# Second-level sums for blocks 3 to 6 of the first layer in the second pair-of-batches pass, and a new instruction sequence

## The chip, the core and the metric

The kernel runs on one core of one Trainium2 chip. A core has a matrix engine (TensorE, PE in the profile, with its weight loads shown as PEld), a vector engine (VectorE, DVE), an activation engine (ScalarE, ACT), a general engine (GpSimd, POOL) and a queue that issues transfers (SyncE, SP). Each engine runs its own instructions in order and waits on semaphores for the others. The metric is the time of one execution on the device, in microseconds. The kernel before was timed in three runs, 1473.35 to 1478.22 us, median 1473.81.

## What is computed

Attention with normalised queries and keys, and then a two-layer product with a bilinear middle, all in float32:

```python
# q, k, v: (8, 12, 448, 64)
q_n, k_n = rmsnorm(q, g_q), rmsnorm(k, g_k)
scores = q_n @ k_n.T / sqrt(64)
attn = softmax(scores)
x = (attn @ v).transpose(0, 2, 1, 3).reshape(8 * 448, 12 * 64)   # 3584 x 768
a = x @ w_a                # 768 -> 1536
b = x @ w_b
out = (a * b) @ w_out      # 1536 -> 768
```

## The kernel before

**Attention.** Twelve heads of eight batches are taken in 24 steps p, each with four heads (in the code a step is a pair of head pairs). `loads` fetches q, k and v (line 424), `normalize` makes the root mean squares (lines 462, 464, 497, 499 on ACT, DVE and POOL), `transposes` turns k and q on TensorE (530) and copies them to a tile "qkT" (548, 550), `scores` multiplies and exponentiates (588, 594) into tiles "ET", `values` multiplies with v (610), `add_up` and `sums_over_keys` make the denominators (624, 646), and `invert` and `divide` apply them (696, 739). The result of a step is written into tiles "x", the input of the two-layer product. There are nine such tiles, four "ET", two "qkT", and one or two each of "q", "k", "v", "sq", "sum", "rec" and "qn".

**The two-layer product** runs over four passes beta = 0 to 3, each of two batches (896 tokens). The matrices are cut in 2 x 2 quarters, and seven products of sums of quarters take the place of eight plain ones. The sums of the weights' quarters are made once, in pass 0, and kept in DRAM ("kept" and "kept_o"); those of x are made by `combine`. The first layer is made in 12 units: six blocks m = 0 to 5 of 128 columns, each with ab = 0 (w_a) and 1 (w_b).

In passes 0 and 1 a unit is `quarter_products`: seven sums times three TensorE products of 448 columns (line 1295, tile "pq"), whose results are taken out of PSUM by ACT and DVE (1317 to 1352) and multiplied on POOL (1343, 1355). The unit's factors, 1.376 MB, are read from "kept" into one of two tiles "st" (393).

In passes 2 and 3 the first layer is `deep_products` instead: each of the seven products is cut once more, in 11 TensorE products of 224 columns (line 872, tiles "da" and "dg"), for w_a and w_b of a block together. A step (m, f), one of 6 x 7, needs factors from "kept" and from "kept_s"; three transfers fetch them (850 to 852) into one of four slots in the two "st" tiles. Sums of x's blocks, "dT" (835), stand in the four "ET" buffers, "sum", "rec" and "qn" for the whole layer; results are gathered in "dF" tiles (885, 891, 911, 912, 919, 924), which stand in the buffers of "q", "k", "sq" and "v", are summed (895) and multiplied (900) into "hT".

What "kept_s" holds is made by `deep_factors` (807): while pass 1 has both units of a block in "st", DVE makes five tiles "ds" of 896 columns in "ET" buffers, and SP writes each to DRAM (809).

The second layer of each pass is `last_product` (line 996, tile "po"), in passes 2 and 3 partly `inner_products` (1193). Its factors come from "kept_o" (395), and its results leave through "o_sb" or "oi" (1368). In pass 1, `inner_factors` makes factors for the later passes too (1132, 1134).

**What sets the order.** Every operation is recorded in a plan with what it reads and writes. `Plan.run` issues them in a fixed sequence, the string `ORDER`, which was made outside the kernel and keeps every operation behind what it depends on. Names such as "held", "ended", "deep factors" or "firsts1" are hints (`HINT`) and make no wait on the chip. The recording order matters where buffers rotate: a tile takes over the buffer of an earlier one of its kind. `PREP` is pass 1, `ONCE` pass 2, `DEEP` holds passes 2 and 3, and `HELD` is attention step 15, the first whose result finds no free "x" tile until pass 1's first layer is done.

In the profile the first output products of pass 0 stand near 407 us, pass 1's first layer from 524 to 717, pass 1's second layer beside attention steps 15 to 23 until 942, pass 2 until about 1196 and pass 3 after it.

Of the kernel before, what the change touches and what calls it, by code (L numbers as in the profile page):

```python
# [12 lines left out]
FP32 = mybir.dt.float32  # L13
# [7 lines left out]
def _float_of(bits):  # L21
# [11 lines left out]
    "c-rkZ33OFOmba>2z4y1bzrW_^X9WZi2#d0afb@VOwk)Hl;0^%=5+ETV3JD;KU}OzzfUt>S6SF|r6PB<f5kWR-MYcw9qaDHNwx@ee-<JfTTYE-5"  # L33
    "<D8xztA4%r>ej8h)xEdw7dtU}6~u~YLMZWqYI@CpMNGpoOt0b(7{qAjRdnpCg1-egK!(^^o)~b03)}(cl;Gq5I3AtQrk|8;!dSy-k=3_FX7dNl"
    "jE8!{nfKGu(|Vp9K}MwZ0G13e2nNHzXP<*-pMmV0oXNX#VA8mWTfHkLY=+V|td*|=&o9Vdx(@y`bN%AXg@sV~1~?b2qzelmZ|Sn7B=65K5@ydD"
    "`G*nnVMgAZuVBWk+^e}uKZhlsuD+7H^3@fKSHiOM%Q(@O<ewEjIAeaW7S5=r3-eCGi8XZ2>#L!VxU1KY<$qpIVEM8?EZf_5@7HjB=e1qsuzmUg"
    "vg7KGt;V*Basj69DuqzVE+AW9K7+EA!YMd)@^~>EJ67Z@ehW6O1K7BB_XcstH+y&NfonT%FW<&V*;V*rJ3wg}S%F)Z7cJkk_2S!Sw{P=Qmz_C$"
    "x~%Nv;Z2nXkHOJ5;hjGo+51i9#yxxXUf;9lz=M0gtlWQf&wKkeR%|>`0p)LB{Al;?YB=0#{h^%)cOE#sVaNXc>-QhqcWB?ygOxEgl{NdS_nkis"
    "hqn7bEIVkF?XQGg@-EMwU2uIj?EGTK?>+;e<daWIoBXMyj9j_AWy_`Omo9C&^5vD^esS^h;)}(fd}^M*qMrZwf_(n+N3P2kN~KHZN<U-gzWDIN"
    "D<2mZfBb>^+m9}NbNSMx*rJQSDK2_%^Xapj&wWtzzFGAC`z7a#E_yB%U2v3~J$Lr#2Sr6kjvYT;bmGJ}CyyTg_oAAk*RCD;ebK)a)m#hzuI9^A"  # L40
    "XHI=qZGL*9>SR^%yN3@SK6?Jhx#RB~K6dnQO-<3M>i?)YRQ2xftE#K3e)H8=iPcr_)fClK7kzp{Ir!<pw<`7hZymjG0$|fID2K|8u=DiJ>XT4$"
    "ctyoKaHOLAdO4KuKGX!(9RR=+DuX?jYsxAvZYeqc(W=YmHm_3muPVXK%g+>-6a#U?_VrtrmTg#Dco5beT6=Kq7FYtGFW$Io$zoWy7>r8*^XHvg"
    "Na@@KbLYPYr`P2XI6env!K|4ubH>{axb|8u<i1L#PX~Zk046Iruw@clfC;V%<6%5xL-sg)7)I8ZEP%|6EK1YU(?_RMnl=guj7SAY84kmTnI?fD"
    "L$YDWU`l}ue2xG-^E5pD6g>4LJoN<9?%y9ChyIU3KX^p;JPduIZy)H>8=%)i@DLb10eZmwJ;;58bnk{rLDzfX-Y(FkGjt(_aW_B*Xy2|~2hx_@"
    "1#o8@fYz;`RZD1@1W7F{q}~*6Z%UdF()c!ebAv=kOn`)VNI=0O0MX%aI6|Xn=o}3NDS+R%9(-N^%LEg2T}J{shChHSCnpDTAbUbKj4Ob#OUH_1"
    "VeCsU6XTeWl{xk$@x_cW85zRpbPzCJ(JsPEFnsv%S94#5P1A>sXG2Axsi|2b(nqAF4jGY}vLrM0?a3J_DKH@|W%$Ao!(rawVZ#O|zmRMV88jFM"
    "4H`HBhUW|(n>-{r`MJTF$<GahLC@$<r#!0+8>a9%{P|e}h75R8?w>rM|6@;iwm<sh#77^0`0>a3Ir|NGq_4AY9~o`=i05HJ==Vb3K0@!_LhtUq"
    "9_rrx*Fw*3&paSW{hsL8PwLv$A@R<fcj?syI`!z%sZ;m+I(6&TrE{l_y*d_j?AYlZ;clTr_YU`U_*J)Gb?DZ$Lx(P1x^(E)`Cqzr?%c)Q{+{;5"
    "?skIaYUdK=QFn<BM@#X(=3?_^f^=^S-n0{M(vbs`SlhOY3D_Zt3X~ASY6m0|r~L)Ms67<4IEXm@1QZ0O5k_zH>&*L=5M^0G%1o0}%2e$PqcTHs"
    "*hFTCT;wq#uZ$MB5X*%?fH3A4m`S`AGwc*^cShDAJ5F_uSP?FS5f_mK!RP0K7cq&+bUL|?B~m7}VygBmHMI^JiVjg4vKTcjlTlqCcLVufkv`!D"  # L50
    "ZnEcL#I)Z5pC4(Ml$g4K(V!BrJ8BE4yw2imqu?V(V8KvOVE$%|d3|Un3v79HK~ah9`6CIt-QN)Mhp!2}CP{=T?CLm=fQ(4`sFd^+GGgRVl98H1"
    "&OA@Z3ull%9SqOHz-I<R)pJmF2o4;Cqm`#<B|Rio9o^gi$iDqGk5^RDYBXK{gP39;dAz|RpKPtzD(vRMmd(Pp507lyTw1od^u0c%rw$0ckN0`^"
    "UCuZ4dh^Y9Hg2ryCH(s9l9K)FcI<_s3bLWFCs|*zcIyLW7YbqZxgKkZ#Wia-t%g%;VCBkpw>j2seP{K`)hl0LxnkAw$`#8Gu2{Yf3f8SHcw>7("
    "VPRSKH!gQ8C94Q@UAbuWq7552EL*>>_rj%1dgmWmvaEDTe$~=d1#jik%EdH4zoKH^qTP!Z&Fc#DSHZlzy!Bg_u3NEe`Letvd2>!JUa~lU_1q<k"
    "7A;@2qNbqJvVvumuwX&{0+_#W{;q{H=WoAf9+bTXn`f8I&dpsg^X?gWuf8^S?wt8+U+*wGZ~EP{XHK7fctyd?yO&O*`7>$xjP`lcb6=S~dDhfU"
    "Q(h~5rFhDesne!SnmlQ0VPS_UbmHoct6rWsvE$V7ujEc?H)&e_<ViV`U(P9?H!*J#%bqZP{9O~qPtBp(lcsFUp1k4Z?1|Zh6S8x%?_9O&rLiks"
    "LXWv~OjcITm@(rPjUSgiu6*3MaWm%5p3!z@=8W7sGp4`Qdd!PilgEq^AZttpj7m?>O)vN;{l#hN`B|9@&y8*~|Lo{_X=$UzjvV=7){7&@jD%Ol"
    "W<u&{Ou8^JJtHkGJ$+BgsLZsK%(V23(Jj+zhF6b*W{?W0L!n8Np+lY@oG~~#Ic-#0@~Gsr5y`2kxRRQZGAOl4%D|!622Q&JQ{2Mrrt@#ZqNU-$"
    "CmK#1@N`2V^J#b@9TG<k7&%~g|6%=yCc?0Icp)L~`9Xsoj;DPYjXW7kAq?Tiq8`0JItoH02oUu5^grN7hi}ioYusrVos4?`OikB7#RyP6NuCxS"
    "k9xc3uG-uRs?#Z>Pewf4iJK(KIle4Vl?IA6M@dqB(Y~-@s#uh1c3oyErlzQk6%#8oElJZ=OH~Xdpdi4PWN5mMKYQvk_11=^D~6#271ghpdK>&S"  # L60
    "OhpZAilQ63ua&O&6(8=4G9rel>j7Q2n(J1SsR#YK?rnu2uVRD^O$n-oY50s5s%5FB8qou)r76A^hNdc-qG_tnr>m-_>Sl8#<X04>t%`J2#Ri4("
    "9W<5J$P<~F(a74T>rt&OpXD=j!wex`pVeA7{d$a1$4ynS0@W<7nWY#ZMGK(HN|NDI?7g_4`c|5%s<zbXX0{53)*59uBFGWh1vI;O^)*)_MwVqL"
    "5#5W3E&YbBgjLhjL)e3=sW&(9p{Qu8TG<q@(p2jaLIP+|%eJJYMJZ@It=7~nmF5QWS5?1VG`CTF8qxG<T~=fpL-r}M*OUXd%d)2V+gJuZHME&&"
    "XnsGcqG>I3*;J!cSqUp<$V^fUuW8AuEc+E%w(zaUs@~*nJy0#%`k)PyRM|k<NLsE{Pd0T~m(_@jy2+L-8_i?{g)~hzeP&BjAMI0RHH5}PbLlOK"
    "A*iZbSKW$$TwH$Q(VR|&Yuq8Z6N%x}Dfci@6&op{!{rb)Q4(cA;_`!{$R(Z2T!|$Ov_zuD$i(j<#N~ELnnWbQLs$bs;z?W_iH#*Z5{bkT5);9^"
    "9VF$UKwR5k=WvkvX=2N$=y0<@R3ID(#s>XyG(asPMWPHVK4{z#<fKW!AMkU(SB=DZ4a*97Rnrhqc81B{rxK5>Bzk1Gi9>NmC4}9E+anvqaw#so"
    "AtMeq@kq?$aJob$Nut*!d0pJ4aSfb_4H(|Cu}Tbg;6)}dPN;peVlflP1g9Xhvu|6014wvf;El^zD?(WV$wA{KDOM6&iP3UQOhAloFB0x2K{e?0"
    "JA77@6><>C%b1?Tn4uYx7IeyPh5(nt?O>`?a&YcW6kXh*q9I)(=ez-P36iJ^f-DFQy!9G!j)qo{B~v7KV~H~dHw;`u09Q~}hZ&CyMCRsNV;6Ty"
    "E{@yrl6NqN<Y*`fPQo}-P-cmX4MjIMIDSw}9}49f6&&`ZEJsV6y0Jc>tf4?T<%rI)5}~{i?z8V_g-X1!D7u|4&Z#8fT=1x>!_&ZFI9#Graymqm"
    "iJ~~1Q66z_r|!nog&j9bROEu2N^dwD+Qou{VIAV3RKn_{5i*kmB^MECQ$%!%q9jRzi1aCSGwPvk2i0RKRXH*i8*%Cs&}xbxaHp%^Z2~fNB2$qu"  # L70
    "50hMtBnj2#g2)6sL!{tDZgIAPD1wtZIBkfeMNU0+THS`#4T!p3z34<C=)#E>abdMURir9$;$cqal$ac0UvMWA8(oo@C^0lBMFrek^fVC7Q=*F!"
    "k;ojW2*j>67>{sLP9>Zm2Zk<SFHk4hh%V?7Xd+rxB}BICEDQoEo=BW4h{ZTZH%(v;DvAPk2~SanFo4w>j7At9&~OozN<<az$0OwEn7olFI$ciP"
    "wjxbp#6_Cd5w%^|L1|d@5Vw<<4zwB-o3%hwxCn8?6OusU;}c?HFc=*?j*!?G+!r8`kUu^?==1qnwD3iOcldpwCV?RFhW-91e=ryoxx?!V`(ymR"
    "C_l4&{@8e5j1`G^V=Sw46uZY~n*IQ>;z)vJ#bCF*x*0G7je?f!HMBUdnP3K@6HIC{B}yYvh8m=b;rA+*8Ba8~-xG~@j^<N>iHha5b1UX{J(Q#c"
    "v}T&p%&TZYs@*2UX?X9c_DvBoH5cYOOLgfk681SmYKY3j=i_dV*x2AMg9%!^lz`zA(n!D=#T`D@82zFlp1Ok8ry&|7B;Y233!|2?gct^(L`aB$"
    "1MgS|a06TdV4S&J0B+0%3`1YAGXU150tmI$soe<t!!`1~pFfQZ`GJgn)Y{)J{$wV0qdx|I3y{*AfZ9{7<%It{?7trNqjpN{K}hYR_6>G~*}oeD"
    ">`^-*b=Ws>Y2EHR2-Hn$G3&m`cWM6>i+UorF5PT@3!wGDdiHf(NWDT(&&UP|H}*oUgm6>BTS-IxraJj30J(MBw}i>JM!WeSH{j%!17zPl)bE4-"
    "X!ri-YV;=|&|6)Zeh(HpcYTA}QHMlpcimWn`pi}bruBHVo^pM>++3tLkiLc1%W;#}Up4qUaC(y&+z<<Ha;CS+@U1BHzqAScyIw-R3nV|qzsOJZ"
    "Q9}M3Wb#u&f&4)E$j==`KUZ9me^kMKY5!~q_WxxgKU*M?UxM<N_J2NC(Eo*aBmcv3@-s!(FG2fD`{C^`Cf^JG"
# [68 lines left out]
def kernel(  # L148
# [35 lines left out]
    nc = tc.nc  # L184
# [90 lines left out]
    def fast_body(ld, wk, ps_s, ps_o, ps_mm, dram):  # L275
# [14 lines left out]
        DEEP, PREP = (NB - 2, NB - 1), NB - 3  # L290
# [474 lines left out]
        def firsts(beta):  # L765
            names = names_of(beta)
            key = 1e4 + beta * 1e3
            h = tile_of(f"h{beta}", "hT", 1)

            def open_h():  # L770
                hTs[0] = wk.tile([P, KO, 2, S], FP32, tag="hT", name="hT")
            op(None, 0.0, 0, open_h, [], [f"{h}/{m}" for m in range(KO)] + [f"{h}/open"], new=[h])
            if beta in DEEP:
                deep_products(beta, key, names, h)
                return
            for n, (m, ab) in enumerate(order):
                if beta:
                    stream(beta, n)
                    st, at = f"st{beta}.{n}", (beta, n)
                else:  # L780
                    st, at = f"st{n}", n
                quarter_products(beta, key, m, ab, st, at, names, h)
                if beta == PREP and ab:
                    deep_factors(beta, m)
# [7 lines left out]
        def deep_factors(beta, m):  # L792

            st, ts = [f"st{beta}.{2 * m + ab}/0" for ab in range(2)], {}
            w = lambda ab, c: (lambda: sts[beta, 2 * m + ab][:, :, c * P:(c + 1) * P])
# [3 lines left out]
            for n, x, y, alu, reads in ((0, w(1, 0), w(1, 1), ALU.add, []), (1, made(0), w(0, 0), ALU.subtract, [0]),  # L799
                                        (2, w(0, 0), w(1, 0), ALU.subtract, []), (3, w(0, 1), made(1), ALU.subtract, [1]),  # L800
                                        (4, w(0, 2), w(1, 2), ALU.subtract, [])):
                nm = tile_of(f"dk{m}.{n}", "ET", 4)

                def emit(n=n, x=x, y=y, alu=alu):
                    ts[n] = wk.tile([P, 2, S], FP32, tag="ET", name="ds", bufs=4).rearrange("p a b -> p (a b)").rearrange(
                        "p (f n) -> p f n", f=7)
                    nc.vector.tensor_tensor(ts[n], x(), y(), alu)
                op("DVE", 1.05, -0.5, emit, st + [f"dk{m}.{x}" for x in reads], [nm, "deep factors"], new=[nm], lock=True)
                op("SP", 0.43, 0, lambda n=n: nc.sync.dma_start(kept["s"][:, m, :, n], ts[n]), [nm], [f"ks{m}.{n}"], kb=434)

        def deep_products(beta, key, names, h):
# [30 lines left out]
            def step(m, f, F, names_F):  # L842
# [64 lines left out]
                if m == f == 0:  # L907
                    rest_of_a()
# [665 lines left out]
```

## Time and profile before

| | us | share |
|---|---|---|
| median of three runs | 1473.81 | |
| the profiled execution, on the device | 1477.19 | |
| its span, first to last instruction | 1475.2 | 100% |
| PE busy | 1452.8 | 98% |
| PE weight loads busy | 944.5 | 64% |
| DVE busy | 998.3 | 68% |
| ACT busy | 438.1 | 30% |
| POOL busy | 332.6 | 23% |
| mean DMA rate over the span | 167 GB/s | |

The profile is of one execution and lists for each engine when it worked. Matmuls are pipelined and their ends are modelled, so busy time of PE says that it was not waiting for long, not that it ran at its peak. A float32 product appears as two records. A row of the groups names a line of the code, the engine, the tiles, the shape and the number of instructions, their busy time and mean duration.

### The profile page before, as it was taken

How to read it: one execution, taken by the hardware profiler on the slowest of the kernel's cores; microseconds unless marked ns; L12 is line 12 of the kernel's file. 1: busy time of each engine (PE TensorE's matmuls, PEld its weight loads, DVE VectorE, ACT ScalarE, POOL GpSimd, SP SyncE). 2: the span in 40 equal slices, each digit the busy share in tenths (PEclk: the TensorE clock that was granted, in tenths of full speed). 3: DMA queues.
4: the chain of work that ended last, by engine and by line, in shares of the span. 5: the costliest groups of instructions: out<-in, count | busy, mean ns of one | idle time of the engine just before them, and what ended most of it. 6: DMA issues, size and time to landing. Idle time of an engine off the chain costs nothing.

```text
span 1475.2 us, 21710 instructions
## 1 busy us (share of the span) xinstructions
PE 1452.8 (98%) x8222; PEld 944.5 (64%) x8222; DVE 998.3 (68%) x1575; ACT 438.1 (30%) x792; POOL 332.6 (23%) x175
## 2 busy tenths in 40 slices
PE   7999999999999999999999999999999999999998
PEld 5433434555444555555544445799997899999898
DVE  4998699888675233344668776466677676666785
ACT  5887752111554000000257770011111011111100
POOL 3456632102233001110255650011210001121000
PEclk9999999999999999999999999999999999999999
DMA  8876467554442555556555635555554755555355
GB/s 222 243 232 173 128 170 224 187 175 170 140 124 82 166 162 168 185 150 179 170 161 143 153 99 169 174 159 154 165 156 162 268 180 169 150 165 175 129 190 152
DMA packets 188884, 248.02 MB, mean 168 GB/s; under 512 B 62564, under 2 KB 161380, under 8 KB 182116
## 3 DMA queue, kind: packets, MB, share of 16 engines
q1 hardware_dynamic: 159652, 192.61, 45.3%
q10 hardware_dynamic: 29120, 53.94, 10.8%
q8 instruction: 67, 1.10, 0.3%
q14 instruction: 45, 0.37, 0.1%
HBM read 188.35 MB, written 57.93 MB: 167 GB/s over the span
## 4 chain that ended last, share of the span: by engine, by line
PE 87%; DVE 5%; DMA 3%; ACT 2%; issue 1%; SPq 0%; POOL 0%; ACTq 0%; DVEq 0%
PE pq L1295 24%; PE dg L872 17%; PE po L996 17%; PE sc L588 6%; PE o L610 6%; PE da L872 6%; PE a L1193 2%; PE g L1193 2%; DMA k_sb<-in_k_dram 1%; PE su L646 1%; PE pt L530 1%; PE b L1193 1%; PE e L1193 1%; PE d L1193 1%; DMA q_sb<-in_q_dram 1%
## 5 line engine op out<-in xcount | busy, mean ns | idle before, releaser
L1295 PE MATMUL pq<-x,st 128*128 128x448 f32 x1008 | 385.1, 541 | 3.3 <-DVE hT L1348 1.3
L1295 PEld LDWEIGHTS pq<-x,st 128*128 128x128 f32 x1008 | 189.5, 190 | 192.8 <-issue 174.4
L594 ACT ACTIVATE ET<-sc,ms 128x448 f32<-128x448 f32 x336 | 191.5, 638 | 88.8 <-PE sc L588 65.9
L499 POOL TENSOR_TENSOR ms<-ms,expo 128x14 f32<-128x14 f32 x47 | 146.6, 3120 | 104.1 <-DVE ms L497 95.0
L872 PE MATMUL dg<-dT,st 128*128 128x224 f32 x672 | 166.5, 353 | 0.1
L872 PE MATMUL dg<-x,st 128*128 128x224 f32 x672 | 164.8, 354 | 0.9 <-DVE dF L919 0.9
L996 PE MATMUL po<-st,hT 128*128 128x384 f32 x492 | 164.1, 488 | 0.0
L588 PE MATMUL sc<-qkT 64*64 64x448 f32 x1344 | 154.1, 545 | 3.4 <-ACT ET L594 2.1
L610 PE MATMUL o<-ET,v_sb 64*64 64x448 f32 x1344 | 149.7, 541 | 0.0
L900 POOL TENSOR_TENSOR hT<-dF 128x448 f32<-128x448 f32 x42 | 47.3, 1139 | 428.1 <-DVE dF L895 428.1
L996 PEld LDWEIGHTS po<-st,hT 128*128 128x128 f32 x492 | 92.4, 190 | 66.9 <-issue 6.5
L872 PEld LDWEIGHTS dg<-x,st 128*128 128x128 f32 x672 | 126.1, 190 | 4.3 <-DVE dF L919 3.6
L872 PEld LDWEIGHTS dg<-dT,st 128*128 128x128 f32 x672 | 126.3, 190 | 2.2 <-DVE dt L912 1.1
L624 POOL TENSOR_TENSOR sum<-sum,ET 128x896 f32<-128x896 f32 x40 | 90.2, 2254 | 131.8 <-DVE sum L624 70.0
L872 PE MATMUL da<-x,st 128*128 128x224 f32 x504 | 117.8, 353 | 0.0
L588 PEld LDWEIGHTS sc<-qkT 64*64 64x64 f32 x1344 | 46.0, 132 | 86.5 <-issue 41.3
L610 PEld LDWEIGHTS o<-ET,v_sb 64*64 64x64 f32 x1344 | 50.3, 133 | 72.8 <-issue 65.3
L872 PEld LDWEIGHTS da<-x,st 128*128 128x128 f32 x504 | 94.8, 190 | 0.7
L895 DVE TENSOR_TENSOR dF<-dF 128x896 f32<-128x896 f32 x84 | 92.0, 1098 | 3.2 <-DVE dF L924 0.5
L996 PE MATMUL po<-st,fin 128*128 128x384 f32 x252 | 86.2, 491 | 0.0
L885 ACT COPY dt<-da 128x224 f32<-128x224 f32 x84 | 29.1, 347 | 191.3 <-PE da L872 148.1
L1343 POOL TENSOR_TENSOR hT<-hT,t 128x448 f32<-128x448 f32 x12 | 16.6, 1382 | 292.8 <-DVE t L1341 265.5
(147 smaller groups left out, 1700.0 us busy)
## 6 DMA issues: line engine op xcount, KB each, us to landing
st<-kept_o SPq DMA_DIRECT2D x28, 1152.0 KB
st<-kept_s SPq DMA_DIRECT2D x84, 320.0 KB
kept<-st ACTq DMA_DIRECT2D x12, 1344.0 KB
st<-kept SPq DMA_DIRECT2D x12, 1344.0 KB
st<-kept SPq DMA_DIRECT2D x84, 192.0 KB
ti<-kept_t SPq DMA_DIRECT2D x48, 288.0 KB
kept_s<-ds SPq DMA_DIRECT2D x30, 448.0 KB
v_sb<-in_v_dram SPq DMA_DIRECT2D x48, 224.0 KB
```

The lines of the kernel that those rows point to most:

```text
L499: lambda: nc.gpsimd.tensor_tensor(msf(), msf(), expo[:, 0:2 * NT * (b - a)], ALU.pow), [], names)
L588: nc.tensor.matmul(t[low_high[w], e, 0:S], lhsT=qkTs[p][low_high[e], 1, w * S + j * D:w * S + (j + 1) * D], rhs=qkTs[p][low_high[e], 0, w ...
L594: nc.scalar.activation(E[:, e], scs[p, j][:, e, 0:S], AF.Exp, scale=rs[p][:, 1, 2 * j + e:2 * j + e + 1])
L610: nc.tensor.matmul(os_[p][low_high[e], w, 0:S], lhsT=xs["v", p][low_high[w], e, j * D:(j + 1) * D], rhs=ETs[p, j][low_high[w], e], start=( ...
L624: two[e].tensor_tensor(sums[p], sums[p] if j > 1 else ETs[p, 0], ETs[p, j], ALU.add)
L872: nc.tensor.matmul(to(), lhsT=W(w), rhs=t(), start=not more and k == 0, stop=k == len(terms) - 1, skip_group_check=True)
L885: nc.scalar.copy(part(0), a())
L895: take("DVE", 1.09, lambda: V.tensor_tensor(F[to], F[to], F[other], ALU.add), allF(other), allF(to), lock=True)
L900: lambda: two[e].tensor_tensor(C(i, n), F[g][:, 0:S], F[g][:, S:2 * S], ALU.mult), allF(g),
L996: nc.tensor.matmul(held["po"][:, 0:HALF], lhsT=a[0]()[:, c], rhs=sts[beta, 12 + place_of[f]][:, c], start=(c == 0), stop=(c == MH - 1))
L1193: nc.tensor.matmul(held[bank], lhsT=x()[:, c], rhs=y(c), start=(start and c == 0), stop=(stop and c == MI - 1), skip_group_check=True)
L1295: nc.tensor.matmul(banks[bank][:, 0:S], lhsT=sts[at][:, f, c * P:(c + 1) * P], rhs=quads[x][:, c], start=(start and c == 0), stop=(stop an ...
```

## The change

The first layer of pass 1 keeps `quarter_products` for blocks m = 0 and 1 and takes `deep_products` for m = 2 to 5. The constant `DEEP` becomes a table `LEAST` of the first block that is made deep in each pass:

```diff
-        DEEP, PREP = (NB - 2, NB - 1), NB - 3
+        LEAST = {NB - 3: 2, NB - 2: 0, NB - 1: 0}
+        PREP = NB - 3
```

```diff
-            if beta in DEEP:
-                deep_products(beta, key, names, h)
-                return
-            for n, (m, ab) in enumerate(order):
+            least = LEAST.get(beta, MH)
+            for m in range(least, MH if beta == PREP else 0):
+                factors_apart(m)
+            for n, (m, ab) in enumerate(order[:2 * least]):
...
                 if beta == PREP and ab:
-                    deep_factors(beta, m)
+                    deep_factors(m, [f"st{beta}.{2 * m + x}/0" for x in range(2)], lambda x, m=m: sts[beta, 2 * m + x])
+            if least < MH:
+                deep_products(beta, key, names, h, least)
```

The second-level factors of blocks 2 to 5 can then no longer be made from what pass 1 streams. A new function loads the block's two kept factors once more, in two portions (four and three of the seven), into the two "qkT" buffers, and makes the five sums of each portion:

```diff
+        PARTS = (slice(0, 4), slice(4, 7))
+
+        def factors_apart(m):
+
+            for fs in PARTS:
+                size, fetched = (fs.stop - fs.start) * KH * P, {}
+                names = [tile_of(f"wa{m}.{fs.start}.{ab}", "qkT", 2) for ab in range(2)]
+
+                def load(ab, fs=fs, size=size, fetched=fetched):
+                    fetched[ab] = wk.tile([P, 2, 2 * S], FP32, tag="qkT", name="da", bufs=2).rearrange("p a b -> p (a b)")[:, 0:size]
+                    nc.sync.dma_start(fetched[ab], kept[2 * m + ab][:, fs.start * KH * P:][:, 0:size])
+                for ab in range(2):
+                    op("SP", 0.4, 6.0 * PREP, lambda ab=ab, load=load: load(ab), [f"kept{2 * m + ab}", "held"], [names[ab]], new=[names[ab]],
+                       kb=0.51 * size)
+                deep_factors(m, names, lambda ab, fetched=fetched: fetched[ab].rearrange("p (f n) -> p f n", n=KH * P), fs)
```

`deep_factors` takes the slice `fs` and makes and writes only that part of each sum: 512 or 384 columns in place of 896. `deep_products` starts at block `least`, and a slot's load depends on both portions where there are two. The sums "dT" of pass 1 are hinted to come after the factors:

```diff
-                    op("DVE", 0.385, -0.4, emit, [f"{x}/0", f"{x}/1", "ended" if beta == ONCE else f"{h}/open"] + ([nm] if n else []),
+                    op("DVE", 0.385, -0.4, emit, [f"{x}/0", f"{x}/1", *(["held", "deep factors"] if beta < ONCE else ["ended"] if beta == ONCE else [f"{h}/open"])] + ([nm] if n else []),
```

Because these tiles take the attention's buffers, pass 1's two layers are recorded when attention step 14 is over, ahead of step 15, and no longer after step 11:

```diff
         for p in range(NC + 1):
+            if p == HELD:
+                sums_over_keys(p - 1, None)
+                invert(p - 1)
+                divide(p - 1)
+                firsts(ONCE - 1)
+                lasts(ONCE - 1)
...
-                    if p // (2 * HC) <= ONCE:
+                    if p // (2 * HC) < ONCE:
                         firsts(p // (2 * HC) - 1)
                         lasts(p // (2 * HC) - 1)
```

The string `ORDER` is made anew for all operations of the kernel, 4773 for 4383. With it the order on every engine is another, also in the first part of the kernel, which has the same operations as before.

## What the change does to the time: a prediction

> **What bounds the kernel now.** I read the table of engine busy time by stretches first, then the chain of waits, then the waits of single lines. From 224 us on the stretches look alike:
>
> ```profile
> 224.00:365.00 141.00, 140.70 (x374) 70.71 (x374) 124.64 (x146) 23.82 (x25) 27.73 (x17) 1.00 0.56 192
> ...
> 478.00:525.00 47.00, 47.00 (x146) 27.72 (x147) 11.79 (x21) 1.45 (x4) 0.00 (x0) 1.00 0.57 170
> ...
> 540.00:684.00 144.00, 144.00 (x397) 72.79 (x395) 57.51 (x78) 8.62 (x15) 19.13 (x15) 1.00 0.57 172
> ...
> 718.00:886.00 168.00, 168.00 (x1440) 74.97 (x1439) 126.48 (x171) 112.75 (x191) 86.39 (x35) 1.00 0.54 145
> ...
> 1196.00:1371.00 175.00, 175.00 (x920) 172.46 (x920) 122.78 (x242) 27.83 (x83) 23.64 (x21) 1.00 0.57 170
> ```
>
> The columns are the stretch, its length, busy PE, weight loads, DVE, ACT and POOL with counts, the granted clock, the DMA share and GB/s. The first busy figure equals the length: TensorE never pauses, at clock 1.00. The stretch 540 to 684 is the first layer of the second pair of batches, which the change rewrites; DVE works 57.5 us of 144 there. The chain of waits says the same:
>
> ```profile
> 477.95 46.64 PE po L996 x144
> ...
> 538.83 144.59 PE pq L1295 x384
> ```
>
> 384 records follow each other without a release from any other engine, at 144.59/384 = 0.3765 us. (A product is two records.) So time is TensorE work, and a saving there counts fully unless something else becomes late.
>
> **What is removed and added on TensorE.** Blocks 3 to 6 (m = 2 to 5) lose 4 x 2 x 7 x 3 = 168 products of 448 columns, 336 records: 336 x 0.3765 = 126.5 us. They gain 4 x 7 x 11 = 308 products of 224 columns (line 872: 3 in "da", 8 in "dg"), 616 records. Their price is the stretch 1196 to 1371 above, which is one whole layer of this kind, 462 products: 175.0/924 = 0.1894 us a record, 116.7 us. Sum: **-9.8 us**; with the price of the other chain piece of line 1295 (140.53 us for 372 records, 0.3778) it is -10.2. I take -10. All other TensorE work stands in both.
>
> **DVE, ACT, POOL.** Per block go 11 evictions of 448 columns (0.617) = 6.8 us. In come 14 of 224 (0.385), 7 of 0.618, 7 of 0.384 and 7 wide sums of 1.098 (lines 911, 912, 919, 924, 895) = 20.1 us. Four blocks: +53; 28 block sums of line 835 at 0.39: +11; three last products move to DVE: +2. The 20 factor sums of 896 columns (1.086) become 20 of 512 and 20 of 384 columns; between the rows 0.552 (384) and 1.086 (896) these are 0.69 and 0.55, so 24.8 for 21.7: +3. DVE gains about 69 us of 1475. Where they lie, TensorE has more: about 80 us of DVE in 117 us of the new products (20.1 x 4), as in the two layers that already run so with 175.0 of 175. ACT goes from 3 x 0.53 to 14 x 0.347 us a block, 19 us beside 117. POOL's products stay at three or four a block. This costs nothing; were DVE the limit there, its 122.8 in 175 would already show it.
>
> **The factor stretch.** This is where cover may go. The old layer read its factors once (12 loads of 1.376 MB in 190 us) and wrote the second level's factors (30 of 0.459 MB) beside. Now those of blocks 3 to 6 must be made before their products, because the block sums take the same four "ET" buffers. In the changed instruction order the eight portions begin under attention pair 14, run on beside the last 90 output products of the layer before (line 996), and end in the second of the two old-style blocks. TensorE has there about 12 (attention) + 60 (30 half groups of three output products at 1.94, two attention pieces) + 63.5 (84 x 2 records at 0.378) = 135 us. SP must move in it: 16 portion loads, 11.0 MB; 4 loads "st<-kept", 5.5; 3 of "st<-kept_o", 3.5; 50 writes "kept_s", 13.8; two first slots of the new products, 1.3; outputs and reciprocals, 2.9. That is 38 MB, 281 GB/s, where the page's slices show 82 to 185 between 400 and 700 us. Is that possible? Slices of 1.5 us of the trace:
>
> ```profile
> 541.00:542.50 1.50, 1.50 (x5) 0.76 (x5) 1.50 (x2) 0.53 (x1) 0.00 (x0) 1.00 1.03 283
> 542.50:544.00 1.50, 1.50 (x5) 0.76 (x5) 0.64 (x2) 0.00 (x0) 0.00 (x0) 1.00 1.02 281
> ...
> 559.00:560.50 1.50, 1.50 (x6) 0.76 (x5) 0.00 (x0) 0.53 (x1) 0.08 (x1) 1.00 0.87 351
> 560.50:562.00 1.50, 1.50 (x6) 0.76 (x5) 0.26 (x1) 0.00 (x0) 0.00 (x0) 1.00 0.99 409
> ```
>
> The first two are the "kept_s" writes alone (pieces of 512 bytes): all 16 engines busy give 282 GB/s. The others are one load "st<-kept": 351 to 409, I take 380. So 20 MB of long loads are 53 us, 13.8 MB of writes 49, the slots 4 (302 GB/s, the deep stretch's rate at full share), the rest about 10 (estimate at 290): **116 us of transfer in 135**. It fits, with 19 us to spare.
>
> Here two rules of the Trainium skill, page "DMA: Bandwidth & Descriptors", stand against the row. Its Specifications call 512 bytes enough for line rate and give about 358 GB/s for one core's HBM: the writes would be 38 us, not 49, the sum 105. The measured 282 decides. Its section Bandwidth wants at least 1 MiB for 75% of peak, with 341 GB/s at 1 MB and 138 at 64 KB; this speaks against cutting 1.376 MB loads into 0.79 and 0.59 and 0.459 MB writes into 0.26 and 0.20. If I read 230 and 310 GB/s between its points (an estimate), portion writes (9.2 MB) would take 40 us instead of 33 and portion loads 36 instead of 29: 130 of 135, no room. But the slices above were full over several writes of 0.459 MB in a row, each hiding the next one's start; I take 116 and keep 130 for the range.
>
> **The wait that is added.** A portion's five sums wait for a pair of loads into the two "qkT" buffers, which the portion before holds to its last sum. A load of 1.376 MB issued at 524.61 has its last bytes by 529.3, 4.7 us. A four-seventh pair (1.57 MB) behind two or three writes (0.93 us each) is about 7.5 us and its sums 3.5; a three-seventh pair (1.18 MB, writes of 0.70) 6.0 and 2.8. Four of each: 79 us; the foreign loads that the same queue carries in between are some 38 us, of which about 25 pass while DVE sums. 92 us in the 101 that the order gives from the first to the last portion sum. Behind a waiting sum stand, on DVE, the evictions of "pq" and "po", and TensorE waits for these, with two banks: one product group (2.3 to 3.9 us) of delay is free. Today's such waits are small:
>
> ```profile
> DVE ds L807 <- DMA st<-kept: 2.7, 3, 1.6
> ```
>
> Three waits, 1.6 us at most, and TensorE lost nothing by them. The price is thus from 0 (every load lands within the free group) to eight times a few us, 15. I am near 0, since the row is: **+1 to +2 us**.
>
> **Attention restarts later.** In the old order pair 15 was loaded, transposed and scored inside the old layer; now its buffers (q, k, sq, v) hold the new products until their end. DVE's last work on them is 0.38+1.10+0.38+2x0.55+1.10+0.63 = 4.7 us after TensorE's last; the k load takes 4.4 (issued 518.62, bytes to 523): 9.1. TensorE meanwhile has 24 output products, 24 x 0.648 = 15.5 us (46.64/72). Then transposes 1.3, copy 0.91, square 0.96, sum 1.08, 0.33, root 3.12, two exponentials 1.17 each: the first score bank is free at 24.5, and TensorE asks for it at 15.5+1.3+3.9+1.6+3.9 = 26.2. Covered, by 1.7 us. If the load comes 8 us later, up to 6 are lost. The output products so used are missing later, but total filler is the same, 168, and the stretch 718 to 886 was full. I put +0.5.
>
> **Start.** The new sequence also reorders the first 224 us, at equal counts. There the engines wait for each other; TensorE's recorded idle time is 6 us (0 + 1.7 + 4.4). It can win or lose a few us, between -3 and +4; nearest row says 0.
>
> **Sum.** -10 + 1.5 + 0.5 = -8 on the span: 1475.2 becomes 1467. The profiled execution as a whole took 1477.19, 2.0 more than its span and 3.4 above the median of 1473.81; the median becomes about **1466**.
>
> **Rivals.** (a) *The gain is given back.* Loads land late at several of the eight portions, 1 us or so each, or the restart lacks 3 to 6 us: 4 to 10 us lost, 1470 to 1476. For it: 86% transfer load in one stretch, 9 us of chain slack. Against: three DMA waits today at no loss. (b) *The transfers become the bound there, slower than before.* One mechanism: between attention pair 14 and the first new product 38 MB must pass. TensorE's cover is 135 us plus the 10 gained; below 38/145 = 262 GB/s the kernel is slower. At 240, between the 20 us slice 540 to 560 (209 at 0.74 share, 282 if full) and what small portions could do, it is 158 us: +23 - 10, about 1487. Against: 282 is the worst saturated rate shown. (c) *The start decides*: the reordered first stage costs 4 us more, 1470, or saves 3, 1463. (d) The change does nothing: then 616 records would be absent from line 872's group; the order has them, so I give it no chance.
>
> **Chances.** Forecast (1461 to 1469) 0.62; (a) 0.20; (b) 0.13; (c) 0.05, split between its sides. Within 0.3% (4.4 us) is what a measurement of this kernel cannot tell from no change. Faster takes the forecast and part of (c): 0.64; same takes most of (a): 0.20; slower takes (b) and the end of (a): 0.16. The range 1459 to 1478 leaves out most of (b) and a better start.
>
> **What would show it.** Line 1295's group (its new line number) falls from 1008 to 672 records, the "dg" and "da" groups rise by 616 together. Right: the stretch before the first "dg" keeps TensorE at its length, DMA near 280 GB/s and share about 0.85 there, and waits of the factor sums for "da" loads under 3 us each. Wrong: TensorE idle before "pq" or "po" released by DVE in that stretch, a share near 1.0, or a gap before the score products of pair 15.

## The result and the profile after

| | before | after |
|---|---|---|
| median | 1474.02 us (5 runs, 1473.35 to 1480.18) | 1465.21 us (5 runs, 1463.84 to 1466.43) |
| ratio | | 0.9934, 95% interval 0.9918 to 0.995 |
| span of the profiled execution | 1475.2 | 1463.3 |
| PE busy | 1452.8 | 1441.9 |
| DVE busy | 998.3 | 1060.1 |

The kernel is 8.8 us faster, the forecast was 8. Two terms of the forecast were wrong by about the same amount, with opposite signs, so the closeness of the total is in part luck. First the lines that answer to those of before. The page's costliest groups, with records, busy us, mean ns, and TensorE's idle time before them with its releaser:

```profile
L1318 PE MATMUL pq<-x,st 128*128 128x448 f32 x672 | 258.4, 542 | 5.1 <-DVE t L1359 2.4
L895 PE MATMUL dg<-dT,st 128*128 128x224 f32 x896 | 223.5, 353 | 0.3 <-DVE dt L934 0.3
L895 PE MATMUL dg<-x,st 128*128 128x224 f32 x896 | 219.3, 353 | 0.0
...
L895 PE MATMUL da<-x,st 128*128 128x224 f32 x672 | 157.4, 353 | 0.1
```

"pq" fell from 1008 to 672 records; "dg" and "da" rose from 672, 672 and 504 by 616 together. The last column of the first row is new in kind: 5.1 us before "pq", mostly behind DVE. The busy time by stretches, columns as before:

```profile
445.00:492.00 47.00, 44.83 (x229) 22.67 (x224) 30.95 (x48) 11.75 (x23) 4.60 (x2) 1.00 0.76 240
492.00:519.30 27.30, 27.30 (x85) 16.16 (x86) 9.06 (x17) 0.00 (x0) 0.00 (x0) 1.00 0.98 324
519.30:586.60 67.30, 64.19 (x170) 31.60 (x169) 42.18 (x72) 3.19 (x6) 4.65 (x4) 1.00 0.87 272
586.60:703.60 117.00, 117.00 (x618) 115.90 (x617) 78.15 (x141) 18.77 (x56) 17.87 (x15) 1.00 0.55 164
```

The last row is the new deep part: 117.0 us for its 616 records (308 products), no pause, DVE at 78. The three rows above are the factor stretch. There TensorE is busy 5.3 us less than its length, and the DMA share (second to last column) is 0.98 in the middle row. The mean over the three rows, weighted by length, is 0.85 at 271 GB/s. The chain of waits (start, length, engine and work) goes through a transfer; between 430 and 800 us the chain of before goes through none:

```profile
519.33 9.03 PE pq L1318 x24
...
529.06 4.79 PE pq L1318 x12
...
534.55 12.11 PE pq L1318 x32
546.66 8.01 DMA st<-kept
...
554.81 31.81 PE pq L1318 x84
```

The load of block 2's factors sets the time from 546.66 on; it was issued when block 1's last factor sum, which reads the same buffer, had ended on DVE (546.2). And the waits of the factor sums themselves, on DVE from 440 to 720 us (us in total, times, longest):

```profile
DVE ds L813 <- DMA kept_s<-ds: 3.8, 4, 2.4
DVE ds L813 <- DMA da<-kept: 3.6, 4, 1.3
```

Now the part that the change leaves as it was but for the order, the first 230 us. Before and after:

```profile
0.00:130.00 130.00, 120.72 (x1260) 55.55 (x1260) 103.97 (x126) 97.56 (x154) 61.35 (x28) 0.99 0.80 219
130.00:230.00 100.00, 95.41 (x743) 38.83 (x738) 82.56 (x103) 64.48 (x101) 53.85 (x21) 1.00 0.62 166
```

```profile
0.00:130.00 130.00, 124.80 (x1316) 57.24 (x1320) 106.31 (x131) 101.10 (x161) 63.31 (x29) 1.00 0.85 229
130.00:230.00 100.00, 97.09 (x709) 40.43 (x702) 85.30 (x104) 60.90 (x96) 48.76 (x21) 1.00 0.61 159
```

TensorE's pauses there fell from 9.28 + 4.59 = 13.9 us to 5.20 + 2.91 = 8.1, and the granted clock rose from 0.99 to 1.00. The factor stretch and its surroundings, before and after:

```profile
440.00:590.00 150.00, 149.87 (x586) 78.88 (x583) 59.12 (x83) 22.23 (x39) 20.28 (x11) 1.00 0.48 142
```

```profile
440.00:590.00 150.00, 144.72 (x540) 75.71 (x539) 86.75 (x144) 18.62 (x35) 11.77 (x9) 1.00 0.84 265
```

So the ledger of the two profiled executions reads: start -5.8 in pauses and about -1.2 in clock, TensorE's work -10, factor stretch +5.2 (5.28 us of pauses between 440 and 590 where before had 0.13). Sum -11.8; the spans differ by 11.9. The medians differ by less, since the profiled execution of before took 1477.19 us, 3 more than its median, and that of after 1465.21, its median.

### The profile page after: what moved, and what is told of

Same layout as the page of the kernel before. It is cut to its first block, busy times and chain, and to the rows that moved or that the text cites. A ratio compares the mean times of both kernels' runs of the same rounds, so it can differ in the third digit from the quotient of the medians.

```text
span 1463.3 us, 22732 instructions
## 1 busy us (share of the span) xinstructions
PE 1441.9 (99%) x8502; PEld 997.2 (68%) x8502; DVE 1060.1 (72%) x1722; ACT 449.3 (31%) x836; POOL 335.7 (23%) x176
## 3 DMA queue, kind: packets, MB, share of 16 engines
q10 hardware_dynamic: 29120, 53.94, 10.9%
## 4 chain that ended last, share of the span: by engine, by line
PE 64%; DVE 1%; DMA 1%; issue 0%; POOL 0%; ACT 0%; DVEq 0%; ACTq 0%
PE dg L895 23%; PE po L1019 13%; PE da L895 9%; PE pq L1318 4%; PE sc L592 3%; PE o L614 3%; PE a L1216 2%; PE g L1216 2%; PE d L1216 1%; PE b L1216 1%; PE e L1216 1%; PE pt L534 1%; DMA st<-kept 1%; PE su L650 0%; POOL ms L503 0%
## 5 line engine op out<-in xcount | busy, mean ns | idle before, releaser
L1318 PE MATMUL pq<-x,st 128*128 128x448 f32 x672 | 258.4, 542 | 5.1 <-DVE t L1359 2.4
L895 PE MATMUL dg<-dT,st 128*128 128x224 f32 x896 | 223.5, 353 | 0.3 <-DVE dt L934 0.3
L895 PE MATMUL dg<-x,st 128*128 128x224 f32 x896 | 219.3, 353 | 0.0
L1318 PEld LDWEIGHTS pq<-x,st 128*128 128x128 f32 x672 | 125.7, 190 | 134.2 <-issue 115.7
L895 PEld LDWEIGHTS dg<-dT,st 128*128 128x128 f32 x896 | 168.5, 190 | 3.9 <-DVE dt L934 1.0
L895 PEld LDWEIGHTS dg<-x,st 128*128 128x128 f32 x896 | 168.7, 190 | 3.0 <-DVE dF L942 1.9
L895 PE MATMUL da<-x,st 128*128 128x224 f32 x672 | 157.4, 353 | 0.1
L918 DVE TENSOR_TENSOR dF<-dF 128x896 f32<-128x896 f32 x112 | 124.2, 1113 | 3.3
L914 ACT COPY dF<-da 128x224 f32<-128x224 f32 x112 | 38.7, 346 | 176.2 <-PE da L895 138.3
L628 DVE TENSOR_TENSOR sum<-sum,ET 128x896 f32<-128x896 f32 x60 | 65.2, 1087 | 32.5 <-POOL sum L628 18.4
```

The lines of the kernel that those rows point to most:

```text
L628: two[e].tensor_tensor(sums[p], sums[p] if j > 1 else ETs[p, 0], ETs[p, j], ALU.add)
L895: nc.tensor.matmul(to(), lhsT=W(w), rhs=t(), start=not more and k == 0, stop=k == len(terms) - 1, skip_group_check=True)
L914: nc.scalar.copy(F[f][:, 0:HS], a())
L918: take("DVE", 1.09, lambda: V.tensor_tensor(F[to], F[to], F[other], ALU.add), allF(other), allF(to), lock=True)
L1318: nc.tensor.matmul(banks[bank][:, 0:S], lhsT=sts[at][:, f, c * P:(c + 1) * P], rhs=quads[x][:, c], start=(start and c == 0), stop=(stop an ...
```

## The experiments

**Start and deep blocks apart.** The first 980 places of the sequence hold the same operations in both kernels, so their order can be exchanged alone; nothing else is edited:

```
ORDER:  places 1 to 980 as in the other kernel, the rest as it was
```

> The kernel before, with its first 980 operations (everything up to about the middle of the first pass's second-level stage) put into the order that the changed kernel has for the same 980; nothing else differs. Theory A (the gain is TensorE work of blocks 3 to 6, the new start is worth nothing): 1474 us as before, within 1.5. Rival S (the 5.3 us by which the changed kernel's profile is ahead when the second pass starts are real and come from the order of the start): 1469 us.

> The changed kernel with its first 980 operations put back into the order of the kernel before. Theory A: 1465 to 1466 us, as the changed kernel. Rival S: 1470.5 us, only 3.5 below the kernel before.

The kernel before with the new start took 1471.2 us (ratio 0.9973, 0.9958 to 0.9987); the changed kernel with the old start 1470.59 (0.997, 0.9954 to 0.9987). The kernel before, beside them, 1474.39. So the new start alone is worth about 0.27% or 3 to 4 us, the deep blocks with the old start 0.30% or 4 us, and together they make the changed kernel's 0.66%. Theory A is refuted; rival S said 2.2 us too much for the first run (1469) and met the second (1470.5), and each part is about half of the gain. The pauses follow the start's order, not the deep blocks: 8.9 us in the first 230 us with the new start in the kernel before (130 - 124.23 + 100 - 96.90), 12.0 with the old start in the changed kernel. First the new, then the old start:

```profile
0.00:130.00 130.00, 124.23 (x1300) 57.30 (x1304) 104.64 (x130) 100.00 (x158) 62.13 (x29) 1.00 0.84 227
```

```profile
0.00:130.00 130.00, 122.88 (x1252) 56.37 (x1252) 103.33 (x126) 96.61 (x153) 61.34 (x28) 0.97 0.80 217
```

The worth of the start is less sharp than the medians say. Of the 23 executions of the kernel before beside these, 10 took 1477.5 to 1480.8 us, at a granted clock of 0.997 to 0.998, and none of the 12 with the new start took more than 1473.6. Against the other 13 alone (median 1472.6) the new start gains only 1.4 us in the kernel before, while in the changed kernel it gains some 5.

**More and fewer bytes in the factor stretch.** All 40 portion writes twice, 20 of them twice (the condition is then `size < 7 and n % 2 == 0 and (n < 4 or fs.start)`), or none:

```diff
+                def write(n=n):
+                    nc.sync.dma_start(kept["s"][:, m, fs, n], ts[n])
+                    if size < 7:
+                        nc.sync.dma_start(kept["s2"][:, m, fs, n], ts[n])
```

```diff
+                    if size == 7:
                         nc.sync.dma_start(kept["s"][:, m, fs, n], ts[n])
...
-                    nc.sync.dma_start(W(5, 5), kept["s"][:, m, f].rearrange("p n c -> p (n c)"))
+                    nc.sync.dma_start(W(5, 5), kept["s"][:, m % 2, f].rearrange("p n c -> p (n c)"))
```

> The changed kernel with each of the 40 portion writes of second-level factors issued a second time, to another buffer that nobody reads: 9.2 MB more in the factor stretch, at the measured 282 GB/s 32.5 us more of transfer. Theory A by its own sum (116 us of transfer in 135 us of TensorE work): 148 in 135, so about 13 us slower than the changed kernel, 1478 us. Rival B1 (the transfers of the stretch are the bound already, as the share of 1.0 between 490 and 565 us suggests): 28 to 32 us slower, 1494 us. Rival B2 (the order of waits sets the time there, not bytes): at most 5 us slower, 1466 to 1470 us.

> The changed kernel with 20 of the 40 portion writes issued twice (4.46 MB more, at 282 GB/s 15.8 us of transfer). The full dose of 9.2 MB cost 19.6 us, of which the trace shows 10.6 as more idle time of TensorE and 4.6 as a lower granted clock. Theory A (there is room for some 15 us of transfer, and beyond it each us counts): 0 to 4 us slower than the changed kernel, 1465 to 1469 us. Rival B1 (the transfers are the bound already, the dose counts in proportion): 9 to 10 us slower, 1475 us.

> The changed kernel without the 40 portion writes: blocks 3 to 6 read the second-level factors of blocks 1 and 2 in their place, as many bytes from other addresses, so the output is not the reference's. 9.2 MB less in the factor stretch. If the 5 us that TensorE stands there between 445 and 587 us come from transfers (theory A with a small price, or B1): 3 to 5 us faster than the changed kernel, 1460 to 1462 us. If they come from the order of the operations on the vector engine (B2): 1464 to 1465 us.

> The changed kernel once more, on the same chip as the next three, as their measure: 1465 us, within 1.5.

The changed kernel again took 1465.9 us (0.994). Half the dose took 1475.02 (1.0002, 0.9987 to 1.0018), 9.1 us more; the full dose 1484.8 (1.0065, 1.0039 to 1.009), 19 to 20 more; no writes 1464.65 (0.9931, 0.9908 to 0.9954), which is not to be told from the changed kernel. Per added MB that is 2.0 to 2.1 us at either dose, some 60% of what the bytes need alone at 282 GB/s (3.5 us per MB). The full dose met none of its three expectations (13, 28 to 32, at most 5 us), the half dose met B1, whose 9 to 10 us were scaled from the full dose, and the run without writes met B2. Not all of the cost is waiting: in the profiled executions TensorE's pauses between 440 and 590 us grew from 5.3 to 12.2 us with the half dose and to 15.9 with the full one, and the mean granted clock was lower (0.998 and 0.994 against 0.999). Still, with the half dose the added pauses alone (6.9 us) exceed the 0 to 4 us that a free room of 15 us allows. The share from 490 to 565 us shows why, first in the changed kernel, then with all writes doubled, then without them:

```profile
445.00:490.00 45.00, 44.30 (x227) 22.64 (x223) 29.04 (x45) 11.75 (x23) 4.60 (x2) 1.00 0.75 235
490.00:565.00 75.00, 70.41 (x197) 36.82 (x196) 38.63 (x69) 2.66 (x5) 3.43 (x3) 1.00 0.98 319
565.00:590.00 25.00, 25.00 (x77) 14.27 (x76) 17.87 (x29) 0.88 (x2) 3.59 (x3) 1.00 0.64 179
```

```profile
490.00:565.00 75.00, 63.65 (x165) 33.31 (x163) 30.90 (x52) 1.60 (x3) 0.00 (x0) 0.91 1.03 324
```

```profile
490.00:565.00 75.00, 72.66 (x204) 38.24 (x203) 37.22 (x68) 2.66 (x5) 3.44 (x3) 1.00 0.67 231
```

The engines are full for 75 us and have room only ahead of it and behind it. Room at the ends took a part of the added bytes (with doubled writes the share rose from 0.75 to 0.82 ahead and from 0.64 to 1.02 behind), the rest delayed TensorE. With doubled writes a second cost came: the granted clock of 0.91. Without writes the share is 0.67, yet TensorE still pauses 3.0 us there (of 5.3): the bytes were not all that held it.

**The order of products.** The timeline of TensorE in the changed kernel shows each piece that began after a pause, in brackets the pause and its releaser:

```profile
491.97 27.36 PE L1019 MATMUL po<-st,hT 128*128 128x384 f32 x84 [1.48 <-DVE fin L1090]
...
529.06 4.78 PE L1318 MATMUL pq<-x,st 128*128 128x448 f32 x12 [0.71 <-DVE hT L1356]
534.55 13.80 PE L1318 MATMUL pq<-x,st 128*128 128x448 f32 x36 [0.71 <-DVE hT L1362]
549.07 4.78 PE L1318 MATMUL pq<-x,st 128*128 128x448 f32 x12 [0.71 <-DVE t L1359]
554.81 31.81 PE L1318 MATMUL pq<-x,st 128*128 128x448 f32 x84 [0.97 <-DMA st<-kept]
```

Three pauses of 0.71 us: in the new sequence the two halves of a sum (twice in bank d: B12, then B22; once in bank g) follow each other at once, and the second waits until DVE has read the first out of the same bank. The old sequence had another bank's product between them. Two exchanges in `ORDER` put it back; a second kernel also mended the places at 491.97 and 554.81 by moving one eviction and one factor sum forward on DVE:

```
block m = 0, ab = 0:  a b a d d g g   becomes   a b a d g d g
block m = 0, ab = 1:  a b a g d d g   becomes   a b a d g d g
second kernel too:    "fin" (491.97) ahead of the two "x" divisions, block 1's last "ds" ahead of a portion's
```

> The changed kernel with two pairs of products exchanged in the first block of the second pass, so that the two halves of the sum in bank d no longer follow each other at once (another bank's product stands between them, as in the kernel before). Theory O (the three waits of 0.71 us there are the order of the products: each second half must wait until the first half has been read from its bank): the three waits go, 2.1 us faster than the changed kernel, 1463 us. Rival V (the vector engine is late there because of the added factor sums, so the wait comes back at another product): at most 0.5 us faster.

> As the run before, and two more places mended: the vector engine takes the eviction of the output product at 491 us ahead of a multiplication that waits for a reciprocal's load, and the last factor sum that reads block 1's first factors goes ahead of a portion sum, so that the load into that buffer can start 0.7 us earlier. If those waits (1.48 and 0.97 us) are the vector engine's order: another 1.5 to 2.2 us, 1461 us in all. If they come from bytes in the queue (the transfers): they move to the next product, 1463 us.

Both theories missed: 1465.12 us (0.994) and 1465.06 (0.9934), at most 0.8 us gained against 1465.9 and nothing to be told from 1465.21. Rival V, the wait that comes back at another product, is what came. The pauses moved. TensorE's waits from 440 to 800 us with the exchanges, and with all four mended:

```profile
PE pq L1317 <- DMA st<-kept: 1.7, 1, 1.7
PE po L1018 <- DVE fin L1089: 1.2, 1, 1.2
PE pq L1317 <- DVE t L1358: 0.9, 1, 0.9
PE pq L1317 <- DVE hT L1361: 0.7, 1, 0.7
```

```profile
PE po L1018 <- DVE o_sb L1041: 2.0, 2, 1.5
PE pq L1317 <- DVE t L1358: 0.9, 1, 0.9
PE pq L1317 <- DVE t L1374: 0.9, 1, 0.9
PE pq L1317 <- DVE hT L1361: 0.7, 1, 0.7
```

One 0.71 is gone, and the wait for the load grew from 1.0 to 1.7; where "fin" was mended, the next output tile "o_sb" waits in its place. In the kernel before, the place of the remaining "hT" pause, behind the layer's first six groups of three products, held the transposes of step 15's k (538.04 to 538.69), which the change moves behind the layer. If full transfers stand behind a late DVE, pauses would move in this way. The test of that is to take both limits away:

> The changed kernel without the 40 portion writes (factors of blocks 1 and 2 read in place of those of 3 to 6, so the output is not the reference's) and with the two exchanges of products of the run called swaps. Alone each gained at most 1 us. If the two limits stand behind each other (what one frees, the other takes): both together 3 to 4 us faster than the changed kernel, 1461 to 1462 us, and TensorE idle between 440 and 590 us falls from about 5 to 1 to 2 us. If the vector engine's own work is what is left: 1464 to 1465 us, as either alone.

1462.44 us (0.9911, 0.9899 to 0.9924), 2.8 to 3.5 us faster than the changed kernel, where the parts alone gave at most 1.3 and 0.8. By the times alone this is little more than the two added; the pauses say it more clearly. Between 440 and 590 us they are 5.3 us with the exchanges alone, as in the changed kernel, 3.0 without the writes alone, and 1.2 with both:

```profile
440.00:590.00 150.00, 148.80 (x566) 80.97 (x565) 87.23 (x147) 19.87 (x38) 11.95 (x9) 1.00 0.65 214
```

All three waits of 0.71 us are gone here, though the exchanges are the same. So two limits stand one behind the other: the transfers of the stretch and the order of its first products.

**Another queue for the writes.**

```diff
-nc.sync.dma_start(kept["s"][:, m, fs, n], ts[n])
+(nc.scalar if size < 7 else nc.sync).dma_start(kept["s"][:, m, fs, n], ts[n])
```

> The changed kernel with the 40 portion writes issued from the scalar engine's queue, which has almost nothing to do between 478 and 590 us; same bytes, but the loads on the sync engine's queue no longer stand behind writes that wait for the vector engine (42 us of such waits between 440 and 590 us). Theory Q (the 4 to 5 us that TensorE loses there are the order in the one queue): 2 to 5 us faster than the changed kernel, 1461 to 1463 us. Rival B1 (all sixteen engines are full from 490 to 565 us whatever the queue): 0 to 1 us faster; and loads that now run beside the writes could delay the buffers of the sums, up to 3 us slower.

1469.31 us (0.9975, 0.996 to 0.9991), with a wide spread (1466.96 to 1479.51): some 4 us slower. Theory Q is not borne out: taking the writes out of the one queue gained nothing. Its profiled execution was the fastest of its runs, with 5.6 us of pauses in the stretch, and doesn't show where the slower ones lose. Their mean granted clock is lower (0.994 at 1479.51 us against 0.999 at 1466.96, some 7 of the 12.6 us between them); what drew it there, and the rest, stay open.

**The restart of attention.** The load of k for step 15 was put behind four small stores of "kept_t" (the expectation says five) and a load of v:

```
SP before the edit:  k15  kt kt v15 kt kt      v16 q16
SP with it:               kt kt v15 kt kt k15  v16 q16
```

> The changed kernel with the load of k for attention pair 15 issued behind five small stores and a load of v, about 7.5 us later than now (issued at 707.2 us, then near 715). Theory of the prediction (the restart is covered by only some 1.7 us and up to 6 of the next 8 are lost): TensorE waits 4 to 6 us for k at the transposes, the kernel is 3 to 6 us slower than the changed kernel, 1468 to 1471 us. Rival R (the cover is wider than worked out, since the load lands within some 5 us of its issue and the transposes come at 719 us): 0 to 1.5 us slower.

1469.68 us (0.9972, 0.996 to 0.9983), 3.8 to 4.5 us slower. The load was issued 12.9 us after the last deep product instead of 3.8. TensorE at the transposes:

```profile
722.97 0.24 PE L533 MATMUL pt<-ident,k_sb 64*128 64x64 f32 x1 [0.46 <-DMA k_sb<-in_k_dram]
...
724.78 1.01 PE L533 MATMUL pt<-ident,k_sb 64*128 64x64 f32 x13 [1.57 <-DMA k_sb<-in_k_dram]
```

Only 2.0 us of the 9.1 are waits: the cover at the transposes is about 7 us. Most of the rest is again the clock, 0.71 in the five us from 725 on (1.5 us). The third group of scores came 30.3 us after the last deep product instead of 26.4, the 4 us that the medians show.

**More work on the vector engine.** Two evictions of each new product done twice, in pass 1 alone:

```diff
-V.tensor_tensor(F[f][:, HS:S], part(1), bank(1, 1)(), ALU.add)
+[V.tensor_tensor(F[f][:, HS:S], part(1), bank(1, 1)(), ALU.add) for again in range(2 if beta == PREP else 1)]
```

The eviction of 448 columns is doubled in the same manner.

> The changed kernel with two of the four evictions of each new product in the second pass's first layer done twice (the same values written again): 28 x (0.62 + 0.38) = 28 us more of the vector engine in the stretch of 117 us where it now works 78. Theory of the prediction (the vector engine's work there costs nothing while it stays under TensorE's): 106 of 117 us, 0 to 1.5 us slower than the changed kernel. Rival (banks are released late well before the vector engine is full): 5 us or more slower.

1478.66 us (1.0042, 1.0026 to 1.0059), some 13 us slower than the changed kernel again. In the deep stretch TensorE did 568 records in the 118 us in which it had done 620, with DVE busy 94 of 118:

```profile
588.00:706.00 118.00, 113.06 (x568) 104.83 (x567) 94.42 (x179) 17.48 (x52) 15.82 (x14) 1.00 0.50 150
```

And from its waits in these 118 us:

```profile
PEld dg L894 <- DVE dF L941: 11.4, 22, 1.1
```

DVE is far from full, and TensorE stands all the same: the weight loads of the next product into a bank wait for the eviction of that bank, which now takes 0.62 us longer. This prices an eviction that grows longer, not DVE work in another place; that was not run.

## Why the prediction was right

Time, sign and range held. The mechanism held for TensorE's work and the restart; the factor stretch was priced too low and the start was given no gain, and these two errors cancelled by luck. The steps one by one:

- **TensorE's work, -10.** Right. The records are those counted, the deep stretch took 117.0 us for a forecast of 116.7, and PE's busy time over the span fell by 10.9 us, of which about 1.2 is the clock at the start.
- **DVE costs nothing.** Right for this change (+61.8 us for +69; 117.0 of 117.0 busy in the deep stretch). The reason given, that DVE would be a limit only near full, is refuted by the doubled evictions: at 94 of 118 us they cost some 10 us of the stretch.
- **Factor stretch, +1 to +2.** Mis-sized: pauses of 5.3 us against 0.13 before, and the deep blocks with the old start gained 4 us instead of 8. The mean came as forecast (0.85 of the engines' time, 271 GB/s), and the portion sums' waits for their loads stayed at 1.3 us or less. What failed is "116 us of transfer in 135, with 19 us to spare": the room is not in one piece. It lies before 490 and after 565 us, and between them the engines are full. The dose shows it: room of 15 us would have made the half dose cost 0 to 4 us; it cost 9. Nor is it bytes alone: without the portion writes 3.0 us of pauses remain, and the order of the first products, which the prediction did not price, holds the larger part of them. The sign named for a wrong step, TensorE idle before "pq" and "po" released by DVE, was there, in the page's group of "pq".
- **Restart, +0.5.** Right, and the cover was wider than worked out for k itself: no pause, the third group of scores asked for at 729.81 - 703.42 = 26.4 us (forecast 26.2), and 7 us of slack at the transposes. The sentence on a later load (up to 6 lost of 8) gave the right size, 4 us, but only 2 of it are the wait; the clock makes most of the rest.
- **Start, 0 (from -3 to +4).** Wrong: -3 to -5. The step read 6 us of pauses in that part (0 + 1.7 + 4.4) and so left little to win. Its 0 stands for the first stretch, where TensorE works 32.46 of 40 us:

```profile
0.00:40.00 40.00, 32.46 (x310) 20.49 (x314) 21.45 (x30) 22.23 (x33) 13.83 (x13) 0.96 0.92 227
```

After the change it works 37.21 there. Between 0 and 230 us the pauses of before are 13.9 us. Rival (c) put a gain at -3 and gave it little chance.

So the sum -10 + 1.5 + 0.5 + 0 = -8 was met by about -10 + 5.3 + 0 - 4.5 = -9: two errors of some 4 us each that happened to cancel. Rival (a) (4 to 10 us given back) is what the deep blocks did: without the new start the kernel would stand at 1470.6, inside the time that (a) gave. Rival (b) was not reached, but it was near: 4.46 MB more and the whole gain is gone. Of the start, it stays open which of the many exchanged places made the gain. No version that computes the reference's output beat the changed kernel.

## What to carry to other kernels

A stretch that must move many bytes is judged by its fullest part, not by its mean: cut it into slices of 5 to 10 us, and where several in a row show full DMA engines, count added bytes as time (here 2 us per MB). Where two limits stand one behind the other, mending either can show next to nothing; try both together before you drop a cause. A re-made sequence is a change of its own, and its worth is measured by putting the other order into the part that the kernels have in common.

## What was not expected of the hardware

**A short pause of TensorE can cost twice.** With half the dose TensorE paused 3.07 us at 511; slices of 1 us (busy PE first, the granted clock third from the end):

```profile
511.00:512.00 1.00, 0.00 (x0) 0.00 (x0) 0.00 (x0) 0.00 (x0) 0.00 (x0) 1.00 1.13 367
512.00:513.00 1.00, 0.00 (x0) 0.00 (x0) 0.00 (x0) 0.00 (x0) 0.00 (x0) 1.00 1.18 422
513.00:514.00 1.00, 0.00 (x0) 0.00 (x0) 0.58 (x2) 0.00 (x0) 0.00 (x0) 1.00 1.00 401
514.00:515.00 1.00, 0.97 (x2) 0.65 (x3) 0.90 (x2) 0.00 (x0) 0.00 (x0) 0.63 1.00 365
515.00:516.00 1.00, 1.00 (x3) 0.42 (x2) 0.00 (x0) 0.00 (x0) 0.00 (x0) 0.50 1.11 434
516.00:517.00 1.00, 1.00 (x3) 0.59 (x2) 0.00 (x0) 0.00 (x0) 0.00 (x0) 0.50 0.97 399
517.00:518.00 1.00, 1.00 (x3) 0.53 (x2) 0.00 (x0) 0.00 (x0) 0.00 (x0) 0.66 1.02 346
```

Half the clock for some 3.5 us, 1.7 us of work lost on top of the pause. The same kernel paused 2.72 us at 492 and 3.17 at 557 without it, and the late k load drew it with two pauses of 0.46 and 1.57 us. The Trainium skill, page "TensorE: Matmul & The Clock Gate", Part 1, tells of two states, half and full clock, judged over a free-running window of about 3.4 us. The half and the length agree with these rows, and a window that runs free would explain why one pause draws it and a like one doesn't; but pauses of 2 to 3 us sufficed here, less than a whole window, and that the window is the reason is not shown by these runs. It may also bear on the start: the profiled execution of before had a pause of 3.78 us near 28 us and a clock of 0.73 from 30 to 35 us, and that of the changed kernel with the old start a pause of 1.91 us near 44 and a clock of 0.72 from 45 to 50. With the new start neither is there, and the runs of the changed kernel lie closer together (1463.84 to 1466.50) than those of before (1471.42 to 1481.95). That the clock is what sets those runs apart was not tested.

**Long loads and short writes together** moved 319 GB/s at a share of 0.98 in the changed kernel (490 to 565 us) and 324 at 1.03 with all portion writes doubled. The write-only slices of before gave 282, the loads 351 to 409.
